# The seam of a two-phase ConvNeXt V2 block: other sums for the last block, another order for the second phase

## The chip, the cores and the metric

The kernel runs on one NeuronCore of a Trainium2 chip. The metric is device time in microseconds (us) of one execution, the median of several. A lower number is better. The profile is of one execution, taken by the hardware profiler.

Engines: PE (TensorE, matrix products), ACT (ScalarE, here GELU), DVE (VectorE), POOL (GpSimd) and SP (SyncE, here a queue that issues DMA transfers). PE writes to PSUM, the accumulator memory of eight banks; the others read from there and from SBUF.

## What is computed

A ConvNeXt V2 block on a 512 x 512 image with 96 channels in bf16: a depthwise 3x3 convolution, a layer norm over channels, an expansion to 384 channels with GELU, a global response norm (GRN) and a projection back, with the input added.

```python
out = zeros_like(x)                       # depthwise 3x3 with zero padding
for i in range(3):
    for j in range(3):
        out = out + xp[:, i:i+H, j:j+W, :] * dw[i, j]
h = _layernorm(out, axis=-1)
h = gelu(einsum('bhwc,ce->bhwe', h, w1))
gx = sqrt((h * h).sum(axis=(1, 2), keepdims=True) + 1e-6)
nx = gx / (gx.mean(axis=-1, keepdims=True) + 1e-6)
h = grn_gamma * (h * nx) + grn_beta + h
return x + einsum('bhwe,ec->bhwc', h, w2)
```

The GRN needs, for each of the 384 expanded channels, the sum of squares over all 262,144 pixels before the projection of the first pixel can be made. That splits the kernel into two phases.

## The kernel before

The image is cut into 128 blocks of 4 rows (2048 pixels). A block has four quarters of 512 pixels. A quarter's expansion is 1536 columns of PSUM, three banks, for 128 partitions.

*First phase.* For each block, in order: convolution on PE, squares, layer norm statistics, the normalised block `yn` written to DRAM and read back as `ynT` (one of six ring buffers, channels on partitions), then the expansion and GELU. The sum of squares of the expanded values is made in one of two ways for each quarter:

- channel-major (`cm_unit`): channels stand on partitions, three matmuls of 512 columns, and DVE takes statistics of each of the three channel chunks (`entry`: one `bn_stats` into the tile `bst`, 32 entries to a group). `aggregate(k)` condenses a group into `mom2` and `tot2`.
- pixel-major (`px_unit`): pixels stand on partitions, six matmuls that cover the same columns, and PE makes products of each 128-column piece with itself ("Gram products", twelve for a quarter) that add up in the tile `gram`. Its diagonal is the sum of squares. These products are kept in a list, `grams`, and `gram_next(n)` emits n of them at a place that suits.

`cm_quads(q)` (line 105) says how many of a block's quarters are channel-major. The expanded values of most blocks are not kept. Three kinds exist:

- "whole" blocks (36): all four quarters channel-major, stored to DRAM (`g_dram`) and reloaded in the second phase (`load_g`);
- "held" blocks (8, among the last 14): they stay in SBUF;
- "made" blocks (84): expanded again in the second phase (`recompute`, line 317) from `yn`, read again from DRAM by `load_yn`, or from ring buffers for the three `KEPT` ones, 122, 126 and 127.

The last blocks, from 114 on, run in `mlp_tail` (line 707), one quarter after the other.

*The seam*, lines 1048 to 1095: the rest of the Gram products, the last group's `aggregate`, `second_moments` (five DVE operations over all groups), four units of recomputation (`advance(4, PRE)`), the sums of the groups, the diagonal of `gram` (three operations, `junk` and `dsum`), an inverse square root by Newton steps on a tile of 128 x 3, the mean over channels through a tiny matmul with `ones_f`, and last the weights of the projection times the scale, `W2s`. Then two units more (`advance(LEAD, PRE)`, LEAD is 6).

*Second phase*, `stage_mm2` (line 340): for each block in `ORDER`, four steps ("subs") of twelve matmuls of 96 columns with `W2s` into one of two output banks, each followed on DVE by the addition of the bias (`o_sb <- PS,B2c`); after each second one DVE also adds the input (`xr`). Between the subs PE runs recomputations for later blocks: after each sub, `pace` (line 392) calls `advance` up to a due number. One such unit is three matmuls into one of two PSUM triples (`banks3`) and one GELU on ACT into a buffer `gr`. `advance` stops at a block that is five or more places ahead (`PRE`), or if three buffers are full: a made block can only be started when the third made block before it has been consumed (`GRB` = 3, `used`):

```python
even = LEAD + (n * NSUB + sub + 1) * total / (NSUB * NBLK)
advance(max(due, even), n + PRE)
```

`ORDER` (lines 180 to 192) mixes the made blocks with the "free" ones, whole and held, two of the first to one of the second. Before the change it begins 122, 116 (held), 126, 127, 117 (held), 1, 2, 0 (whole), 4, 5, 3 (whole), and it ends 119, 125 (held). `load_yn` is issued on SP seven blocks ahead, `load_xr` four and `load_g` up to five blocks ahead on POOL. A whole block's reload needs a buffer that two blocks earlier in a chain has held; the first two use the buffers of the held blocks 116 and 117.

Within the first phase, the seam and the first eight blocks of the second, instructions stay on each engine in the order of the program; later ones may be placed by a scheduler. Lines in the profile are mostly L36, because a helper there issues the instruction; groups are told apart by their tiles.

Of the kernel before, what the change touches and what calls it, by code (L numbers as in the profile page):

```python
# [15 lines left out]
NEWTON_ITERS = 2  # L16
# [41 lines left out]
def kernel(  # L58
# [23 lines left out]
    NBLK = H // GR  # L82
# [13 lines left out]
    def is_held(q):  # L96
        return q in HELD

    def is_whole(q):
        return q < TAIL0 and q % 10 in WHOLE or q == TAIL0  # L100

    def after_whole(q):
        return (q - 1) % 10 in WHOLE

    def cm_quads(q):
        if is_whole(q) or is_held(q):
            return NQ
        if q >= TAIL0:
            return 1 if q >= NBLK - 2 else 0
        return 2 if q >= NBLK - 16 or after_whole(q) or q % 10 in (5, 9) else 3  # L110

    whole = [q for q in range(NBLK) if is_whole(q)]
# [48 lines left out]
    ones_f = consts.tile([128, 128], f32, name="ones_f")  # L161
    B2bc_f = consts.tile([128, C], f32, name="B2bc_f")

    NENT = sum(cm_quads(q) for q in range(NBLK - 2))
    NLAST = cm_quads(NBLK - 2) + cm_quads(NBLK - 1)
    GROUPS = [min(32, NENT - k) for k in range(0, NENT, 32)] + [NLAST]
    NACC = len(GROUPS)
    mom2 = consts.tile([128, NCH, NACC, 2, 3], f32, name="mom2")
    tot2 = consts.tile([128, NACC, NCH], f32, name="tot2")
# [10 lines left out]
    free, rest = HELD[:2], HELD[2:]  # L180
    for i, q in enumerate(whole):
        free.append(q)
        if (i + 1) * len(HELD[2:]) // len(whole) > len(HELD[2:]) - len(rest):
            free.append(rest.pop(0))
    assert not rest
    made_q = KEPT + [q for q in range(NBLK) if not is_whole(q) and not is_held(q) and q not in KEPT]
    ORDER = []
    for i, q in enumerate(made_q):
        ORDER.append(q)
        while len(ORDER) - i - 1 < ((i + 1) * len(free) + len(made_q) // 2) // len(made_q):  # L190
            ORDER.append(free[len(ORDER) - i - 1])
    assert sorted(ORDER) == list(range(NBLK))
    nth_made = {q: n for n, q in enumerate(made_q)}
    SLOTS = [q % NYT for q in KEPT + [NBLK - 5, NBLK - 4, NBLK - 3]]
# [8 lines left out]
    with ExitStack() as p1:  # L203
# [113 lines left out]
        def recompute(q, t):  # L317
            if t == 0:
                grp[q]["g"] = late.gr.tile([128, NQ, NCH, QW], bf16, name="gr")
            cm_unit(grp[q]["g"][:, t], grp[q]["ynt"], t, grp[q]["w1"])  # L320
# [50 lines left out]
        PRE = 5  # L371
        YPRE = 7
        XPRE = 4
        LEAD = 6
# [9 lines left out]
        def advance(target, upto):  # L384
            while made[0] < total and made[0] < target:
                n, t = todo[made[0]]
                if n >= upto or nth_made[ORDER[n]] >= used[0] + GRB:
                    break
                recompute(ORDER[n], t)
                made[0] += 1  # L390
# [152 lines left out]
        def stage_stats(b, halves=(0, 1)):  # L543
            k = batch_of[b]
            b0, n = BATCHES[k]
            for h in halves:
                src = ysq.pop(b) if h else ybf[b]
                for g in range(NG):
                    c0 = (b - b0) * NG + g
                    for i in range(NI):  # L550
                        pe.matmul(S[:, h, c0:c0 + (GR - 1) * n * NG + 1:n * NG],
                                  lhsT=src[:, i, g * 128:(g + 1) * 128], rhs=rowsel[:],
                                  start=False, stop=(i == NI - 1), skip_group_check=True)
# [78 lines left out]
        def stage_turn(k):  # L632
            NT = (BATCHES[k][1] * GR * NG + 31) // 32 * 32
            rt = rtpool.tile([128, NS], bf16, name="rt")
            dve.transpose(out=rt[:, :NT], in_=rns.pop(k)[:, :NT])
            rts[k] = rt
# [45 lines left out]
        bsts = {}  # L682
        ents = {}
        e_ = 0
        for q in range(NBLK):
            if q == NBLK - 2:
                e_ = 32 * (NACC - 1)
            ents[q] = e_
            e_ += cm_quads(q)
        gs = {}  # L690
# [5 lines left out]
        def quarter(b, t):  # L696
            return gs[b][t] if isinstance(gs[b], list) else gs[b][:, t]

        def entry(b, j, m):
            k, e = divmod(ents[b] + m, 32)  # L700
            if k not in bsts:
                bsts[k] = bstpool.tile([128, NCH, 32, 6], f32, name="bst")
            dve.bn_stats(out=bsts[k][:, j, e, :], in_=quarter(b, m)[:, j, :])
# [3 lines left out]
        def mlp_tail(b, get):  # L707
            if b == IN_GH:
                gs[b] = late.gh.tile([128, NQ, NCH, QW], bf16, name="gh")[:]
            elif b > IN_GH:  # L710
                gs[b] = late.gr.tile([128, NQ, NCH, QW], bf16, name="gr")[:]
            elif b in IN_XT:
                gs[b] = g_xt
            elif b == IN_XIN:
                gs[b] = g_xin
            elif not is_held(b):
                while len(sums_only) < 2 * NQ:
                    sums_only.append(ypool.tile([128, NCH, QW], bf16, name="y_bf")[:])
                gs[b] = sums_only[:NQ]
                sums_only.extend(sums_only[:NQ])  # L720
                del sums_only[:NQ]
            else:
                gs[b] = gpool.tile([128, NQ, NCH, QW], bf16, name="g")[:]
            for t in range(NQ):
                cm = t < cm_quads(b)
                (cm_unit if cm else px_unit)(quarter(b, t), ynts[b], t)
                gram_next(12 if len(grams) > 24 else 6)
                if cm:
                    for j in range(NCH):
                        entry(b, j, t)  # L730
                if t == 1:
                    for k in get("turn"):
                        stage_turn(k)
                if t == 2:
                    for b2 in get("stats"):
                        stage_stats(b2)
                if t > cm_quads(b):
                    owe_grams(b, (t - 1) * QC, t * QC)
            for k in get("moments"):
                stage_moments(k)  # L740
            if cm_quads(b) < NQ:
                owe_grams(b, (NQ - 1) * QC, NQ * QC)
            if is_whole(b):
                stores.extend((b, h) for h in range(3))
# [61 lines left out]
        grams = []  # L806

        def gram_next(n):
            for b, c0, j in grams[:n]:
                c = c0 % QC + j * 128  # L810
                v = quarter(b, c0 // QC).rearrange("p j w -> p (j w)")[:, c:c + 128]
                pe.matmul(gram[:, j, :], lhsT=v, rhs=v, start=False, stop=True, skip_group_check=True)
            del grams[:n]

        def owe_grams(b, c0, c1):
            grams.extend((b, c, j) for c in range(c0, c1, E) for j in range(NCH))

        def aggregate(k):
            bst = bsts.pop(k)
            n = 2 * GROUPS[k]  # L820
            v = bst[:].rearrange("p j e (h s) -> p j (e h) s", h=2)[:, :, :n]
            for j in range(NCH):
                dve.bn_stats(out=mom2[:, j, k].rearrange("p h s -> p (h s)"), in_=v[:, j, :, 1])
            dve.tensor_reduce(out=tot2[:, k, :], in_=v[:, :, :, 2], axis=AX.X, op=ALU.add)

        def combine(b):
            for k in sorted(bsts):
                if k < NACC - 1 and (b >= NBLK - 3 or ents[b + 1] >= 32 * (k + 1)):
                    aggregate(k)

        def second_moments(k0, k1):
# [52 lines left out]
        for s in range(last_slot + 1):  # L884
# [73 lines left out]
            else:  # L958
                b = mlp[0]
# [88 lines left out]
        while stores:  # L1048
            store_next()
        gsm = p2.enter_context(tc.tile_pool(name="gsm", side="right", bufs=1))  # L1050
        gram_next(len(grams))
        aggregate(NACC - 1)
        second_moments(0, NACC)
        advance(4, PRE)
        sums = gsm.tile([128, NCH], f32, name="sums")
        dve.tensor_reduce(out=sums[:], in_=parts[:].rearrange("p j k h -> p j (k h)"), axis=AX.X, op=ALU.add)
        for j in range(NCH):
            junk = bstpool.tile([128, 128], f32, name="junk")
            dve.scalar_tensor_tensor(out=junk[:], in0=gram[:, j, :], scalar=1.0, in1=ident_f[:],
                                     op0=ALU.mult, op1=ALU.mult, accum_out=dsum[:, j:j + 1])  # L1060
# [4 lines left out]
        dve.tensor_scalar(out=gi[:], in0=ssq[:].bitcast(i32), scalar1=-0.5, scalar2=float(0x5F3759DF),  # L1065
                                op0=ALU.mult, op1=ALU.add)
        r = gi[:].bitcast(f32)
        for it in range(3):
            t_ = gsm.tile([128, NCH], f32, name=f"gt{it}")
            dve.scalar_tensor_tensor(out=t_[:], in0=r, scalar=-0.5, in1=r, op0=ALU.mult, op1=ALU.mult)  # L1070
            dve.tensor_tensor(out=t_[:], in0=t_[:], in1=ssq[:], op=ALU.mult)
            rn_ = gsm.tile([128, NCH], f32, name=f"gr{it}")
            dve.scalar_tensor_tensor(out=rn_[:], in0=t_[:], scalar=1.5, in1=r, op0=ALU.add, op1=ALU.mult)
            r = rn_[:]
# [17 lines left out]
                                    op0=ALU.mult)  # L1092
        dve.tensor_copy(out=B2c[:], in_=B2bc_f[:])

        advance(LEAD, PRE)
    with p2:
        def out_part(q, o_sb, v):
            r0 = q * GR
# [58 lines left out]
```

## Time and profile before

| | us |
|---|---|
| median of 3 runs | 1434.84 (1434.36 to 1438.47) |
| the profiled execution | 1430.97 |
| its span, first to last instruction | 1429.2 |
| last GELU of the first phase ends | 936.6 |
| first sub of the second phase starts | 944.36 |
| last sub starts, about | 1424.3 |

The first line of the page's part 1 gives the busy time of each engine and its share of the span:

```profile
PE 1378.1 (96%) x23332; PEld 827.4 (58%) x23332; DVE 1304.8 (91%) x2396; ACT 1381.4 (97%) x1693; POOL 887.7 (62%) x735
```

In the second phase the groups by line are, with busy time, mean duration in ns, and idle time before:

```profile
L36 ACT ACTIVATE gr<-PS 128x1536 bf16<-128x1536 f32 x332 | 463.2, 1449 | 12.4 <-PE PS L36 6.3
L36 DVE TENSOR_TENSOR o_sb<-PS,B2c 128x384 bf16<-128x384 f32 x512 | 280.7, 556 | 57.7 <-PE PS L36 52.8
L36 PE MATMUL PS<-ynT,w1s 128*128 128x512 bf16 x972 | 262.7, 379 | 0.0
L36 PE MATMUL PS<-W2s,gr 128*128 128x96 bf16 x4032 | 209.7, 206 | 1.0 <-DVE o_sb L36 0.4
```

[...] Busy shares are averages over both phases, so a place is read from a timeline or a window of that place.

### The profile page before, as it was taken

To read this page: it belongs to the slowest core of one execution; us is meant where nothing else is said; L and a number is where in the kernel's file an instruction comes from. 1 tells how busy PE (TensorE), PEld (TensorE's weight loads), DVE (VectorE), ACT (ScalarE), POOL (GpSimd) and SP (SyncE) were. 2 spreads that over 40 slices of the span, in tenths; PEclk is the share of its full clock that TensorE was granted. 3 is DMA by queue.
4 is the path that set the end of the run, shared out by engine and by line. 5 is a ranking of instruction groups with operands and counts; after the bars stand their busy time and mean duration, and the time that the engine had idled before them with its cause. 6 is when DMAs were issued, how large, how long until landed. Compare 5 with 4: busy or idle time off the path is not lost.

```text
span 1429.2 us, 54985 instructions
## 1 busy us (share of the span) xinstructions
PE 1378.1 (96%) x23332; PEld 827.4 (58%) x23332; DVE 1304.8 (91%) x2396; ACT 1381.4 (97%) x1693; POOL 887.7 (62%) x735
## 2 busy tenths in 40 slices
PE   8899999999999999999999997799999999999998
PEld 3445455545555555554545554367777777777776
DVE  8859999999999999999999998988888888888888
ACT  7899999999999999999999999999999999999996
POOL 3559999999999999999999997302111111111110
PEclk9999999999999999999999999999999999999999
DMA  6577989898998888999889877649999999999996
GB/s 193 174 227 228 274 265 288 263 273 255 283 269 274 260 269 249 267 269 276 271 257 282 262 232 232 198 161 414 419 385 414 401 407 398 413 390 394 395 405 272
DMA packets 167565, 423.64 MB, mean 296 GB/s; under 512 B 34167, under 2 KB 83767, under 8 KB 162711
## 3 DMA queue, kind: packets, MB, share of 16 engines
q1 hardware_dynamic: 151652, 314.59, 69.0%
q0 software_dynamic: 15104, 105.39, 18.5%
q8 instruction: 182, 2.98, 0.9%
q14 instruction: 65, 0.52, 0.1%
q10 hardware_dynamic: 562, 0.15, 0.1%
HBM read 262.16 MB, written 157.79 MB: 294 GB/s over the span
## 4 chain that ended last, share of the span: by engine, by line
PE 58%; ACT 16%; DVE 13%; DMA 6%; POOL 3%; SPq 2%; issue 2%; ACTq 0%; POOLq 0%; DVEq 0%
PE PS L36 58%; ACT g L36 12%; DVE bst L36 8%; ACT y_bf L36 4%; DMA yn_dram<-yn 3%; DVE xT L36 2%; DMA xin<-in_x_dram 2%; SPq L36 2%; POOL ysq L36 1%; DVE o_sb L36 1%; POOL yn L36 1%; DMA ynT<-yn_dram 1%; DVE y_bf L36 1%; ACT ysq L36 0%; DVE mom L36 0%
## 5 line engine op out<-in xcount | busy, mean ns | idle before, releaser
L36 ACT ACTIVATE g<-PS 128x512 bf16<-128x512 f32 (+2 forms) x1160 | 703.6, 780 | 3.7 <-PE PS L36 3.4
L36 DVE BATCH_NORM_STATS2 bst<-g 128x6 f32<-128x512 bf16 x1020 | 623.5, 675 | 23.2 <-ACT g L36 22.5
L36 ACT ACTIVATE gr<-PS 128x1536 bf16<-128x1536 f32 x344 | 479.7, 1456 | 14.0 <-PE PS L36 7.9
L36 POOL TENSOR_TENSOR yn<-y_bf,rbc 128x1536 bf16<-128x1536 bf16 x126 | 391.6, 3110 | 50.6 <-ACT rbc L36 21.4
L36 PE MATMUL PS<-ynT,w1p 128*128 128x512 bf16 x1110 | 341.2, 381 | 16.7 <-ACT g L36 8.7
L36 PE MATMUL PS<-xT,Wq 64*32 64x511 bf16 (+1 forms) x9198 | 336.5, 386 | 12.1 <-ACT g L36 3.0
L36 DVE TENSOR_TENSOR o_sb<-PS,B2c 128x384 bf16<-128x384 f32 x512 | 280.7, 556 | 57.7 <-PE PS L36 52.8
L36 POOL TENSOR_TENSOR ysq<-y_bf 128x1536 bf16<-128x1536 bf16 x114 | 313.5, 2750 | 31.4 <-ACT y_bf L36 22.4
L36 PEld LDWEIGHTS <-g 128*128 128x128 bf16 (+1 forms) x3603 | 217.8, 98 | 119.1 <-issue 37.6
L36 PE MATMUL PS<-ynT,w1s 128*128 128x512 bf16 x972 | 262.7, 379 | 0.0
L295 POOL DMA_DIRECT2D xr<-in_x_dram x116 | 62.2, 536 | 286.3 <-DVE o_sb L36 286.3
L36 PEld LDWEIGHTS <-gr 128*128 128x128 bf16 x4104 | 201.0, 98 | 53.8 <-issue 1.5
L36 PE MATMUL PS<-W2s,gr 128*128 128x96 bf16 x4032 | 209.7, 206 | 1.0 <-DVE o_sb L36 0.4
L36 ACT ACTIVATE y_bf<-PS 128x1536 bf16<-128x1536 f32 (+2 forms) x147 | 184.1, 1274 | 13.0 <-PE PS L36 8.9
L36 DVE STREAM_TRANSPOSE xT<-xin 128x576 f32<-128x576 f32 (+1 forms) x256 | 181.8, 750 | 5.9 <-PE PS L36 4.9
L36 PEld LDWEIGHTS <-w1p 128*128 128x128 bf16 x1110 | 94.9, 97 | 158.7 <-issue 113.8
L36 PEld LDWEIGHTS <-Wq 64*32 64x32 bf16 x9216 | 104.6, 90 | 130.4 <-ACT g L36 61.5
L36 PE MATMUL PS<-g 128*128 128x128 bf16 x1632 | 158.2, 220 | 4.3 <-DVE PS L36 4.1
L36 DVE TENSOR_TENSOR o_sb<-o_sb,xr 128x768 bf16<-128x768 bf16 x256 | 142.8, 558 | 8.9
L36 PE MATMUL PS<-w1p,ynT 128*128 128x384 bf16 (+1 forms) x924 | 141.3, 273 | 7.0 <-ACT y_bf L36 2.0
L36 PEld LDWEIGHTS <-ynT 128*128 128x128 bf16 x924 | 73.0, 97 | 58.4 <-issue 35.5
L36 PE MATMUL PS<-W2s,g 128*128 128x96 bf16 x1968 | 103.7, 206 | 0.2
(114 smaller groups left out, 656.8 us busy)
## 6 DMA issues: line engine op xcount, KB each, us to landing
g<-g_dram POOLq DMA_DIRECT2D x36, 1536.0 KB, 9.8
xin<-in_x_dram SPq DMA_DIRECT2D x126, 432.0 KB
g_dram<-g SPq DMA_DIRECT2D x105, 512.0 KB
yn_dram<-yn SPq DMA_DIRECT2D x512, 96.0 KB
ynT<-yn_dram SPq DMA_DIRECT2D x128, 384.0 KB
out_dram<-o_sb SPq DMA_DIRECT2D x127, 384.0 KB
xr<-in_x_dram POOLq DMA_DIRECT2D x124, 384.0 KB, 7.6
ynT<-yn_dram SPq DMA_DIRECT2D x243, 128.0 KB
```

The lines of the kernel that those rows point to most:

```text
L36: r = f(*a, **k)
L295: pq.dma_start(out=xr[:], in_=x[0, r0:r0 + GR].rearrange("r w c -> (r w) c").rearrange("(p g) c -> p g c", g=PXP))
```

## The change

Four parts, all around the seam:

1. `cm_quads`: block 127 has no channel-major quarter any more; its first quarter goes the pixel-major way too. The last group of statistics, which held one entry each of blocks 126 and 127, is gone; the entry of 126 joins the group before, and that group is aggregated after block 127. `mlp_tail` emits twelve Gram products a quarter for blocks 126 and 127 where it emitted six.
2. The seam is in another order: one unit of recomputation ahead of the second moments and of the last Gram products, then, after these, units up to the third; the fourth stands after `W2s` in the program. Four units are made ahead of the first sub where there were six; `LEAD`, the pace's constant, stays 6.
3. Two Newton steps instead of three.
4. `ORDER`: the two held blocks 116 and 117 come first. The rest is spread anew. It now begins 116, 117, 122, 126, 127, 0 (whole), 1, 2, 3 (whole), 4, 5, 7 (whole), 6, 8, and still ends 119, 125.

```diff
@@ cm_quads
-            return 1 if q >= NBLK - 2 else 0
+            return 1 if q == NBLK - 2 else 0
@@ groups of statistics
-    NENT = sum(cm_quads(q) for q in range(NBLK - 2))
-    NLAST = cm_quads(NBLK - 2) + cm_quads(NBLK - 1)
-    GROUPS = [min(32, NENT - k) for k in range(0, NENT, 32)] + [NLAST]
+    NENT = sum(cm_quads(q) for q in range(NBLK))
+    GROUPS = [min(32, NENT - k) for k in range(0, NENT, 32)]
@@ order of the second phase
+    lead, free = free[:2], free[2:]
...
-        while len(ORDER) - i - 1 < ((i + 1) * len(free) + len(made_q) // 2) // len(made_q):
+        while len(ORDER) - i - 1 < i * len(free) // (len(made_q) - 1):
             ORDER.append(free[len(ORDER) - i - 1])
+    ORDER = lead + ORDER
@@ entries
-            if q == NBLK - 2:
-                e_ = 32 * (NACC - 1)
@@ mlp_tail
-                gram_next(12 if len(grams) > 24 else 6)
+                gram_next(12 if len(grams) > 24 or b >= NBLK - 2 else 6)
@@ combine
-                if k < NACC - 1 and (b >= NBLK - 3 or ents[b + 1] >= 32 * (k + 1)):
+                if b == NBLK - 1 or ents[b + 1] >= 32 * (k + 1):
@@ the seam
-        gram_next(len(grams))
-        aggregate(NACC - 1)
+        assert not bsts
+        advance(1, PRE)
         second_moments(0, NACC)
-        advance(4, PRE)
         sums = gsm.tile([128, NCH], f32, name="sums")
         dve.tensor_reduce(out=sums[:], in_=parts[:].rearrange("p j k h -> p j (k h)"), axis=AX.X, op=ALU.add)
+        gram_next(len(grams))
+        advance(3, PRE)
...
-        for it in range(3):
+        for it in range(NEWTON_ITERS):
...
-        advance(LEAD, PRE)
+        advance(4, PRE)
```

## The prediction

> **What bounds the kernel now.** I read the slices of the page first (TensorE, PE, is at 9 tenths almost throughout, ScalarE, ACT, beside it), then the busy time by windows around the place that the change touches: the end of the first phase and the start of the second. Columns: window, length, busy time with count of PE, weight loads, VectorE (DVE), ACT, GpSimd (POOL), then clock, DMA share, GB/s.
>
> ```profile
> 925.00:937.00 12.00, 9.63 (x107) 7.20 (x106) 12.00 (x27) 11.60 (x9) 0.00 (x0) 1.00 0.61 218
> 937.00:944.00 7.00, 4.80 (x28) 2.16 (x26) 5.69 (x38) 5.82 (x5) 0.00 (x0) 1.00 0.00 0
> 1000.00:1050.00 50.00, 49.91 (x751) 37.54 (x748) 43.28 (x81) 48.50 (x36) 8.58 (x16) 1.00 1.02 415
> 1415.00:1430.00 15.00, 8.37 (x158) 7.08 (x154) 10.63 (x21) 4.08 (x3) 0.00 (x0) 0.91 0.28 107
> ```
>
> From 944 to 1415 PE has no gap (49.91 of 50); ACT is close behind (48.50). So the second phase lasts as long as its PE work, and a time saved or lost at its start reaches the end unchanged. The chain of waits, read next, says the same: it is PE alone from piece to piece, 447 matmuls in 30.08 us.
>
> ```profile
> 933.61 3.56 DVE bst L36 x6
> 937.44 0.24 DVE parts L36
> 939.02 0.64 DVE junk L36 x6
> 946.40 26.76 PE PS L36 x393
> 1035.10 30.08 PE PS L36 x447
> ```
>
> The chain passes over DVE from 911 to 942: the sums of the last blocks (`bst`) run behind ACT, and all scales of the second phase hang on them. The timeline of that stretch (start, duration, engine, what, count, idle before) shows the prices:
>
> ```profile
> 933.52 3.65 DVE L36 BATCH_NORM_STATS2 bst<-gr 128x6 f32<-128x512 bf16 x6
> 936.65 0.84 PE L36 MATMUL PS<-gr 128*128 128x128 bf16 x12 [0.20 <-ACT gr L36]
> 937.08 0.29 DVE L36 BATCH_NORM_STATS2 mom<-bst 128x6 f32<-128x4 f32 x3
> 937.34 1.46 PE L36 MATMUL PS<-ynT,w1p 128*128 128x512 bf16 x6
> 938.18 37.60 ACT L36 ACTIVATE gr<-PS 128x1536 bf16<-128x1536 f32 x27 [1.58 <-PE PS L36]
> 938.94 0.28 DVE L36 SCALAR_TENSOR_TENSOR junk<-PS,ident_f 128x128 f32<-128x128 f32 x1
> 941.26 0.16 DVE L36 SCALAR_TENSOR_TENSOR gt<-gr 128x3 f32<-128x3 f32 x1
> 941.85 0.16 DVE L36 SCALAR_TENSOR_TENSOR gx<-ssq,gr 128x3 f32<-128x3 f32 x1
> 943.15 0.56 DVE L36 TENSOR_SCALAR W2s<-w_sb,sc 128x96 bf16<-128x96 bf16 x3
> 944.36 0.67 PE L36 MATMUL PS<-W2s,gr 128*128 128x96 bf16 x12
> ```
>
> Call three matmuls of 512 columns for one quarter of a block, with their GELU, a unit, and twelve matmuls of 96 columns with W2s a sub. In the gapless stretch a unit follows the next work after 0.643 us of PE and a sub after 0.511. This agrees with the chain: 447 matmuls are 21.4 units and 31.9 subs at the program's ratio of 336 to 512, so 13.8 + 16.3 = 30.1 us. A unit costs ACT 1.345 us (units start at 939.68, 941.03, 942.37, 943.71, each when ACT frees a PSUM triple), with 1.45 from its start to its end. Before the first sub, six units are done.
>
> **The change, part by part.** All times are of the profiled execution: span 1429.2 us, 1430.97 with what lies around it, 3.87 under the median of the runs, 1434.84, to which I add the difference.
>
> *Sums.* Block 127's first quarter is no longer read by DVE: three statistics at 3.65 / 6 = 0.61 us go, and the extra group's three statistics and reduction too. DVE ends block 126's three at 933.22 + 1.83 = 935.05 (the earlier group's aggregation, now larger by one entry, comes behind them). From there to the diagonal sums it needs what it needed from 937.08 to 938.94, 1.86 us: 936.9. PE gets 12 Gram products more (42 columns of time each: 0.69 us from 936.65 to 937.34 for twelve) and six matmuls for three in that quarter at the same columns (0.81 us busy either way, rows at 931.28 and 929.93). In that stretch PE waits 0.19 to 0.53 us per quarter for ACT, whose step is 1.345: a quarter with 12 products, 0.643 + 0.69 = 1.33, still fits, so ACT hides them and I take nothing; without that cover it is 0.7.
>
> *Order at the seam.* PE now runs one unit ahead of the last 24 products. Its PSUM is free when the last but one quarter leaves ACT (936.60 - 1.345 = 935.25), so it runs 935.3 to 935.95, and the products end at 935.95 + 2 x 0.69 = 937.35. Diagonal sums start at 937.5 instead of 938.94: 1.44 earlier, PE now being what they wait for. ACT no longer idles 1.58 us.
>
> *Two Newton steps.* Three operations go, 941.26 to 941.85: 0.59 us. From the diagonal sums to the end of W2s were 943.71 - 938.94 = 4.77 us, now 4.18: ready at 941.7. Units 2 and 3 are done at 938.8 (ACT frees the triple at 936.6 + 1.45), the matmul for the mean of gx at 940.3, unit 4 at 941.05. So the first sub starts at 941.75 instead of 944.36: -2.6 us.
>
> *Fewer units ahead.* Four instead of six: 2 x 0.643 = +1.3 us, made up later on the gapless PE.
>
> *A burst.* The pace is unchanged (line 395: 6.7 units due after the first sub), so three units follow that sub at once. The first runs from 942.25, the second to 943.55, the third needs the triple of the first, whose GELU starts at 942.25 + 0.84 = 943.1 and ends at 944.55: 1.05 us of PE waiting. After the next sub a unit waits for the second GELU (944.45 + 1.45 = 945.9 against 945.7): 0.2. Together +1.25.
>
> *A held pace.* Two held blocks lead, so the first made block's buffer comes free after block 2 instead of block 0, and `GRB` = 3 stops units at 12. Counted through `advance`, subs 1 to 3 of block 2 would bring 1, 1, 0 units and now bring 0, 0, 2. Four subs stand in a row: DVE needs 0.56 for each and 0.56 per pair, while the rows at the end, where only subs are left, show pairs in 1.53 us for PE's 1.02; the two output banks take up part, and I take 0.3 of the 1.0. Then two units, a sub, a unit: it waits for the first GELU (0.84 + 1.45 = 2.29 after that unit's start, against 2 x 0.643 + 0.511 = 1.80): 0.5; the one after it 0.2. Together +1.0. This limit binds nowhere later, by the same count.
>
> *New order.* Blocks stand at other places, with the same work. Reads of yn are issued seven blocks before their block's place. The made blocks now stand up to two places later at the start, while their units' times hardly move: a read's room shrinks from 4.5 to 5.25 blocks to 3.5 to 4.25 for some twenty blocks, and from the middle it is as before. A block lasts (1424.9 - 944.36) / 128 = 3.75 us, so the room is 13.1 us. Packet records of the trace show these reads done 2.5 to 7.9 us after their first packet, which came 2.2 us behind the issue at 949.89. Covered; if not, it is the last rival. Reloads of g land in 8.3 to 11.3 us and have at least four blocks, 15 us, as four of them had before. One third of a read is put early in SP's queue, before the output of block 3; it waits for a unit that runs in block 3's first sub, and that output waits for block 3's end: nothing behind it is late. The order ends with the same two blocks, and units end in the same block: the last ten subs stay.
>
> [...]
>
> **Sum:** -2.6 + 1.3 + 1.25 + 1.0 = +0.95 us, 0.07%: no change that can be told (0.3%, 4.3 us, is what a measurement of this kernel tells from none). 1434.84 + 0.95 = 1435.8. Bounds: if the waits of the burst and the held pace are hidden, -1.3 (1433.5); if the seam gives only Newton's 0.59 and the lost cover costs 0.7, +0.95 + 2.0 + 0.7 = +3.65 (1438.5).
>
> **The rivals.**
> - *The seam's gain is kept* (-1.3, 1433.5): ACT starts 1.58 us earlier and so is ahead when the burst comes. For it: ACT has 1.5 us in 50 to spare. Against: two PSUM triples let it be ahead by two units only.
> - *The change does not shorten the chain* (+3.65, 1438.5): the longer last group or ACT holds the diagonal sums. For it: DVE has 12.00 of 12 busy there. Against: 2.3 us of its work go.
> - *Reads come late* (slower): a yn read that takes over 13.1 us from its issue stops PE at the unit that uses it. Nine made blocks have room of at most 3.75 blocks; 0.5 us each is 4.5, with the seam 1434.84 + 0.95 + 4.5 = 1440.3. For it: DMA share is 1.0 from 960 on, and reloads begin two blocks earlier in the order. Against: 10 us were enough.
> - *Clearly faster* (under 1430.5): the median lies 3.87 above the profiled execution for reasons that the trace does not hold; if some stand at the seam, they may go. In the trace PE idles only 2.2 us of 937 to 944.
>
> **How the numbers follow.** Forecast 0.45, gain kept 0.25, chain not shortened 0.10: all within 0.3%, so same 0.80. Late reads 0.12: slower. Clearly faster 0.08. The three runs span 4.1 us, so a median may lie 2 off. The range reaches 2 to 2.5 us below the kept gain and 1.5 above the unshortened chain, 1431 to 1440; most of the last two rivals is left out.
>
> **What would show it.** In the new profile: first sub near 941.8, 2.6 earlier, behind four units, diagonal sums near 937.5, ACT without its 1.58 us; PE waiting for ACT about 1 us after the first sub, and again some 13 us later after four subs in a row; then no gap up to the end. A PE wait for yn or g after 960, a first sub after 943, or bursts without waits would make the steps wrong.

## The result and the profile after

| | before | after |
|---|---|---|
| median of 7 runs each, us | 1434.71 (1431.73 to 1438.47) | 1441.47 (1435.24 to 1448.29) |
| ratio, 95% interval | | 1.0049 [1.0029, 1.0069] |
| profiled execution's span | 1429.2 | 1438.9 |
| block 126's first GELU starts ("first phase") | 925.45 | 934.02 |
| from there to the first sub | 18.91 | 16.02 |
| from the first sub to the end | 484.84 | 488.86 |

The changed kernel is 0.5% slower; 1441.47 lies above the forecast range of 1431 to 1440. Of the 9.7 us between the two spans 8.6 arise before block 126, where both kernels have the same instructions in the same order on each engine. The rest, 504.88 against 503.75, is +1.1 us.

First the chain of waits of the changed kernel (start, duration, what), at the seam and in the second phase:

```profile
937.16 8.92 PE PS L36 x117
946.10 0.73 DVE junk L36 x6
950.04 2.19 PE PS L36 x15
952.30 1.46 ACT gr L36
984.68 30.08 PE PS L36 x447
```

The seam's chain now goes over PE (the Gram products) to the diagonal sums, no longer over `bst`, and the wait for ACT behind the first sub is in it. The steady stretch costs the same, 30.08 us. Its timeline:

```profile
941.80 1.86 DVE L36 BATCH_NORM_STATS2 bst<-gr 128x6 f32<-128x512 bf16 x3
946.10 0.29 DVE L36 SCALAR_TENSOR_TENSOR junk<-PS,ident_f 128x128 f32<-128x128 f32 x1 [0.62 <-PE PS L36]
949.74 0.56 DVE L36 TENSOR_SCALAR W2s<-w_sb,sc 128x96 bf16<-128x96 bf16 x3
950.04 0.90 PE L36 MATMUL PS<-W2s,g 128*128 128x96 bf16 x12 [0.33 <-DVE W2s L36]
950.77 2.73 PE L36 MATMUL PS<-ynT,w1p 128*128 128x512 bf16 x6
952.30 10.97 ACT L36 ACTIVATE gr<-PS 128x1536 bf16<-128x1536 f32 x8 [1.10 <-PE PS L36]
953.80 0.99 PE L36 MATMUL PS<-ynT,w1p 128*128 128x512 bf16 x3 [0.31 <-ACT gr L36]
961.44 2.50 PE L36 MATMUL PS<-W2s,gr 128*128 128x96 bf16 x48
964.69 10.97 ACT L36 ACTIVATE gr<-PS 128x1536 bf16<-128x1536 f32 x8 [1.41 <-PE PS L36]
```

Counted from 934.02, the diagonal sums start at 12.08 (13.49 before) and the first sub at 16.02 (18.91). Three units follow the first sub, and four subs stand in a row at 961.44, both as counted. New is that the first sub takes 0.90 us instead of 0.67 and six matmuls of the units 2.73 instead of 1.46. For the six matmuls the windows say why (the clock stands third from the end); the sub comes further down.

```profile
946.60:950.00 3.40, 1.82 (x9) 0.69 (x8) 2.54 (x20) 3.04 (x3) 0.00 (x0) 1.00 0.00 0
950.00:953.40 3.40, 3.36 (x18) 1.48 (x18) 0.97 (x4) 2.30 (x2) 0.00 (x0) 0.62 0.00 0
1000.00:1050.00 50.00, 49.92 (x742) 37.36 (x741) 43.23 (x81) 48.47 (x36) 8.99 (x18) 1.00 1.02 417
```

The granted clock fell to 0.62 of full in the 3.4 us behind the first sub, right after a stretch in which PE was busy for 1.82 of 3.4 us.

In the first phase (10 to 925 us), the waits of the two kernels that differ, before and then after (total us, times, longest):

```profile
PE PS L36 <- DVE PS L36: 4.1, 6, 1.4
...
DVE xT L36 <- DMA xin<-in_x_dram: 0.9, 1, 0.9
```

```profile
PE PS L36 <- DVE PS L36: 9.6, 11, 2.4
DVE xT L36 <- DMA xin<-in_x_dram: 7.9, 6, 2.9
```

In this pair of profiles the transposition of x waited for x to be loaded six times instead of once. Nothing in the change touches these loads. What the change does move is memory: with one group of statistics less, `mom2`, `tot2` and `parts` are smaller, and the tiles allocated behind them (`ynT`, then the five `g` buffers of 12,288 bytes per partition, then `bst`) stand 128 bytes lower. `g` moves from byte 47744 to 47616 = 93 x 512.

### The profile page after: what moved, and what is told of

Same layout as the page of the kernel before. It is cut to its first block, busy times and chain, and to the rows that moved or that the text cites. A ratio compares the mean times of both kernels' runs of the same rounds, so it can differ in the third digit from the quotient of the medians.

```text
span 1438.9 us, 55003 instructions
## 1 busy us (share of the span) xinstructions
PE 1383.1 (96%) x23347; PEld 829.1 (58%) x23347; DVE 1302.3 (91%) x2386; ACT 1382.5 (96%) x1693; POOL 887.8 (62%) x735
## 4 chain that ended last, share of the span: by engine, by line
PE 57%; ACT 18%; DVE 15%; DMA 5%; issue 2%; SPq 1%; POOL 1%; ACTq 0%; DVEq 0%; POOLq 0%
PE PS L36 57%; ACT g L36 12%; DVE bst L36 10%; ACT y_bf L36 4%; DVE xT L36 3%; DMA xin<-in_x_dram 3%; DMA yn_dram<-yn 2%; SPq L36 1%; DVE y_bf L36 1%; DVE o_sb L36 1%; DMA rbc<-r_dram 1%; POOL yn L36 0%; ACT ysq L36 0%; ACT gh L36 0%; ACT gr L36 0%
## 5 line engine op out<-in xcount | busy, mean ns | idle before, releaser
L36 ACT ACTIVATE g<-PS 128x512 bf16<-128x512 f32 (+2 forms) x1160 | 704.4, 779 | 9.4 <-PE PS L36 8.8
L36 DVE BATCH_NORM_STATS2 bst<-g 128x6 f32<-128x512 bf16 x1020 | 622.8, 674 | 23.0 <-ACT g L36 22.5
L36 ACT ACTIVATE gr<-PS 128x1536 bf16<-128x1536 f32 x344 | 479.7, 1456 | 15.2 <-PE PS L36 9.2
L36 POOL TENSOR_TENSOR yn<-y_bf,rbc 128x1536 bf16<-128x1536 bf16 x126 | 391.2, 3107 | 61.0 <-ACT rbc L36 21.7
L36 PE MATMUL PS<-ynT,w1p 128*128 128x512 bf16 x1107 | 342.6, 384 | 14.9 <-ACT g L36 6.9
L36 PE MATMUL PS<-xT,Wq 64*32 64x511 bf16 (+1 forms) x9198 | 337.2, 387 | 12.1 <-ACT g L36 3.1
L36 DVE TENSOR_TENSOR o_sb<-PS,B2c 128x384 bf16<-128x384 f32 x512 | 280.3, 556 | 61.4 <-PE PS L36 56.2
L36 POOL TENSOR_TENSOR ysq<-y_bf 128x1536 bf16<-128x1536 bf16 x114 | 313.2, 2747 | 29.1 <-ACT y_bf L36 22.6
L36 PEld LDWEIGHTS <-g 128*128 128x128 bf16 (+1 forms) x3603 | 217.8, 98 | 124.9 <-issue 44.3
L36 PE MATMUL PS<-ynT,w1s 128*128 128x512 bf16 x972 | 262.5, 379 | 0.5 <-ACT gr L36 0.4
L36 PEld LDWEIGHTS <-gr 128*128 128x128 bf16 x4116 | 202.1, 98 | 54.3 <-issue 1.1
L36 PE MATMUL PS<-W2s,gr 128*128 128x96 bf16 x4032 | 210.6, 206 | 1.1 <-DVE o_sb L36 0.4
L36 ACT ACTIVATE y_bf<-PS 128x1536 bf16<-128x1536 f32 (+2 forms) x147 | 183.9, 1273 | 14.6 <-PE PS L36 10.5
L36 DVE STREAM_TRANSPOSE xT<-xin 128x576 f32<-128x576 f32 (+1 forms) x256 | 181.8, 750 | 14.8 <-DMA xin<-in_x_dram 7.9
L36 PEld LDWEIGHTS <-w1p 128*128 128x128 bf16 x1107 | 95.0, 98 | 157.3 <-issue 112.2
L36 PEld LDWEIGHTS <-Wq 64*32 64x32 bf16 x9216 | 104.4, 90 | 131.1 <-ACT g L36 59.5
L36 PE MATMUL PS<-g 128*128 128x128 bf16 x1632 | 158.3, 220 | 9.8 <-DVE PS L36 9.6
L36 DVE TENSOR_TENSOR o_sb<-o_sb,xr 128x768 bf16<-128x768 bf16 x256 | 142.7, 557 | 8.9
L36 PE MATMUL PS<-w1p,ynT 128*128 128x384 bf16 (+1 forms) x930 | 142.6, 273 | 6.4 <-ACT y_bf L36 2.0
L36 PEld LDWEIGHTS <-ynT 128*128 128x128 bf16 x930 | 73.7, 98 | 58.5 <-issue 36.0
L36 PE MATMUL PS<-W2s,g 128*128 128x96 bf16 x1968 | 103.8, 206 | 0.5 <-DVE W2s L36 0.3
```

The costliest lines, as they stand in the source:

```text
L36: r = f(*a, **k)
```

## Experiments

Ratios are to the kernel before, run in the same set; one profile each. `warm` and `order_back` have that one execution alone, so no ratio. "First phase" is as in the table above. "33rd" is the time from the first bias addition of the second phase to the 33rd: 30.85 us in the kernel before.

**Is it the program or scatter? Is it the addresses?** `null_before` and `null_after` are the two kernels again.

> The kernel before, unchanged. What its own scatter is. All theories: ratio to before 1.000 within its interval; first phase (to the start of block 126's GELU) 925 us, as in the profile of before. If the first phase alone scatters by several us between profiled executions of one program, the first phase here is off 925.45 by 2 us or more.

> The changed kernel, unchanged. If its 6.8 us are a property of the program: ratio again 1.003 to 1.007, first phase again near 934 us in the profile. If they are scatter of the first phase that fell on this kernel's runs: ratio 1.000 to 1.002 (the seam's own 1 us), first phase anywhere from 925 to 936.

```diff
 after_pad: changed kernel
     dsum = consts.tile([128, NCH], f32, name="dsum")
+    pad = consts.tile([128, 32], f32, name="pad")
```

> The changed kernel with 128 bytes of unused room per partition behind its small tiles, so that ynT and g stand at the addresses that they have in the kernel before (one group of statistics less had moved them down by 128 bytes). Theory of addresses: the first phase is back at 925 us and the ratio at 1.001. Theory of scatter: the same as the changed kernel's repeat within the intervals. Theory that the seam alone costs it: the same as the repeat.

```diff
 before_shift: kernel before
-    gam = consts.tile([128, NCH], f32, name="gam")
-    dsum = consts.tile([128, NCH], f32, name="dsum")
     gpool = ctx.enter_context(tc.tile_pool(name="g", bufs=5))
+    fin = ctx.enter_context(tc.tile_pool(name="fin", bufs=1))
+    dsum = fin.tile([128, NCH], f32, name="dsum")
+    gam = fin.tile([128, NCH], f32, name="gam")
...
-        warm = consts.tile([32, 32], bf16, name="warm")
+        warm = fin.tile([32, 32], bf16, name="warm")
```

> The kernel before with three small tiles moved behind g, so that ynT and g stand 128 bytes lower, at the changed kernel's addresses. Theory of addresses: first phase near 934 us, ratio 1.004 to 1.006. Theory of scatter, and of the seam: ratio 1.000.

**Which tile, and is it the multiple of 512?** `g_back` and `g_half` put an unused tile of 128 and 64 bytes between `ynT` and `g`; `g_lower` makes `before_shift`'s move in the changed kernel; `after_third` is the changed kernel once more.

```diff
 g_back: changed kernel (g_half: 16 instead of 32)
+    gap = ctx.enter_context(tc.tile_pool(name="gap", bufs=1)).tile([128, 32], f32, name="gap")
     gpool = ctx.enter_context(tc.tile_pool(name="g", bufs=5))
```

> The changed kernel with 128 unused bytes between ynT and g: g is back at its address of the kernel before, ynT stays 128 bytes lower. If g's address makes the first phase longer: first phase 925 to 927 us in the profile, ratio as with both back, 1.0008. If ynT's does: first phase 929 to 934, ratio as the changed kernel's repeat, 1.002 or more. If addresses do nothing and the first batch was scatter, the ratio is anywhere from 1.000 to 1.003, with no tie to the address.

> The changed kernel with three small tiles moved behind g: g (and ynT) another 128 bytes lower, g at 47488, 384 above a multiple of 512. If a multiple of 512 is what is slow: ratio 1.000 to 1.001, first phase 925 to 927 us. If a lower place is what is slow, or this is scatter that the address does not set: 1.002 or more, or no pattern.

> The changed kernel with 64 unused bytes ahead of g: g at 47680, 64 above a multiple of 512. If only the multiple of 512 is slow: ratio 1.000 to 1.001, first phase 925 to 927 us. If slowness fades step by step from 0 to 128 bytes: ratio about 1.0015.

> The changed kernel unchanged, a third set of runs. If g's place at a multiple of 512 bytes makes the first phase longer: ratio 1.002 to 1.005 again, first phase 928 us or more. If the earlier two sets were scatter: ratio 1.000 to 1.001.

| kernel | seam and order | g, bytes above a multiple of 512 | ratio, 95% interval | first phase, us |
|---|---|---|---|---|
| changed | new | 0 | 1.0049 [1.0029, 1.0069] | 934.0 |
| null_after | new | 0 | 1.0022 [1.0006, 1.0038] | 929.7 |
| after_third | new | 0 | 1.0025 [1.0012, 1.0038] | 927.8 |
| before_shift | old | 0 | 1.0024 [1.0008, 1.0041] | 931.4 |
| null_before | old | 128 | 1.0007 [0.9993, 1.0022] | 928.2 |
| after_pad | new | 128 | 1.0008 [0.9993, 1.0023] | 925.1 |
| g_back (ynT low) | new | 128 | 0.9997 [0.9986, 1.0008] | 925.9 |
| g_half (ynT low) | new | 64 | 1.0004 [0.9992, 1.0017] | 927.7 |
| g_lower (ynT lower still) | new | 384 | 0.9990 [0.9974, 1.0006] | 929.0 |

In this table all four sets with `g` at a multiple of 512 lie above 1 with their whole interval; of the five others every interval holds 1. Single pairs overlap, so the weight lies in the pattern: the 35 executions of `null_after`, `after_third` and `before_shift` lie on average 0.23% above the median of the kernel before in their set, the 59 of the five others 0.03%, a difference of 0.20% (2.9 us) with a standard error of 0.04%. The old program with only its addresses changed (`before_shift`) is as slow as the changed one's two repeats; the changed program at other addresses is not slower than the kernel before. So the greater part of the repeated loss follows the place of `g`, not the seam; `ynT`'s place does not matter (`g_back`), and lower is not slower (`g_lower`). `bst` moves too, but it stands at its old place in `before_shift`, which is slow, and at the changed kernel's in `g_lower`, which is not. The sizes expected were larger: 1.003 to 1.007 for `null_after` and 1.004 to 1.006 for `before_shift`. The first phase of a single execution scatters, in the kernel before too (925.45 and 928.2), so that column supports the ratios but carries no verdict: `g_lower` and `g_half` missed the 925 to 927 expected of them. The profiles of the versions below fit in: 924.8 to 927.3 for the six with `g` off a multiple, 929.2 for `st_off`, which has it on one. The first set of the changed kernel, 1.0049, was larger than its repeats, 1.0022 and 1.0025; no run explains that surplus.

The instructions that use `g` take the same time in both places (100 to 900 us: GELU into `g` 685 and 687 ns, statistics from `g` 674 and 675 ns). The transfers differ, though not cleanly: in the packet records of that stretch the 3456-byte packets, of which only the loads of x consist, take 172 to 182 ns on average in the four multiple-of-512 profiles of the table, 164 to 169 in the five others except the first profile of before (177); the slowest twentieth of the 4096-byte ones begins at 368 to 384 ns against 347 to 365. Of the versions below, `st_off`, on a multiple, has 167 ns and `st_mult`, off it, 173. Nor is late x what the slow profiles share: the wait for it is 7.9 us in the changed kernel and 3.9 in `before_shift`, but 1.7 and 0.9 in the two repeats. PE's wait for DVE in the first phase (`PE PS L36 <- DVE PS L36`) separates the four, 5.3 to 9.6 us, from the five others, 3.1 to 4.6; `st_off` has 4.3.

**Which access to g?** The stores of `g` to DRAM are the transfers that touch it in this phase. Their cuts were moved:

```diff
 st_off: changed kernel; st_mult, st_ctl: after_pad, with 192 and 64
-                sp.dma_start(out=g_dram[whole.index(b)][:, h * n:h * n + n],
-                             in_=flat(b)[:, h * n:h * n + n])
+                c0, c1 = [0, n + 64, 2 * n + 64, 3 * n][h:h + 2]
+                sp.dma_start(out=g_dram[whole.index(b)][:, c0:c1], in_=flat(b)[:, c0:c1])
```

> The changed kernel (g at a multiple of 512 bytes), each whole block's three stores cut at 0, 4224 and 8320 bytes instead of 0, 4096 and 8192: two of three start 128 bytes above a multiple of 512. If the stores' start decides: ratio 1.000 to 1.001. If the engines' accesses to g decide: 1.002 to 1.005 as the changed kernel.

> The changed kernel at the old addresses (g 128 bytes above a multiple of 512), stores cut at 0, 4480 and 8576 bytes: two of three start at a multiple of 512. If the stores' start decides: ratio 1.0015 to 1.003, two thirds of the changed kernel's surplus. If the engines' accesses decide: 1.000 to 1.001.

> The changed kernel at the old addresses, stores cut at 0, 4224 and 8320 bytes: none starts at a multiple of 512. Control for the uneven cut: 1.000 to 1.001 by both theories; more would mean that the cut itself costs time (in DRAM too the starts are moved).

Measured: `st_off` 1.0007 [0.9994, 1.0021], `st_mult` 1.0010 [0.9998, 1.0022], `st_ctl` 1.0016 [1.0005, 1.0028]. The control, without a start on a multiple, is the slowest of the three and lies above 1 with its whole interval, so the cut seems to have a price of its own, and the three do not separate the theories. They also break the pattern of the table: `st_off` has `g` at a multiple of 512, cuts its stores as unevenly as the control, and is not slower than it, though the intervals overlap. So what is shown of the place of `g` is shown for the kernels with evenly cut stores, and that the stores' start decides is neither shown nor excluded.

**The parts of the seam.** `warm` fills PE's idle stretch, `order_back` restores the order, both from `after_pad`:

```diff
 warm
         advance(3, PRE)
+        for _ in range(7):
+            pe.matmul(PS[:, 6, 128:512], lhsT=w1p[:, :128], rhs=w1p[:], start=True, stop=True)
 order_back
-    lead, free = free[:2], free[2:]
...
-        while len(ORDER) - i - 1 < i * len(free) // (len(made_q) - 1):
+        while len(ORDER) - i - 1 < ((i + 1) * len(free) + len(made_q) // 2) // len(made_q):
...
-    ORDER = lead + ORDER
```

> The changed kernel at the old addresses with seven matmuls of 384 columns (about 1.1 us, results unused) behind the third unit, where PE idles 1.3 us. If idling there drops the clock: granted clock 1.00 in the 30 us around the seam (0.94 in the three profiles of changed kernels), first sub 0.67 us busy instead of 0.9 to 1.3, the three units behind it with 0.64 us steps, and 488.4 us or less from the first sub to the end instead of 488.9 to 489.2. If the clock drops for another reason: 0.94 again.

> The changed kernel at the old addresses with the second phase's order of the kernel before; all else as changed. Theory of the held pace: the wait near block 2 (four subs in a row, then a unit that waits for ACT) is gone, 1.0 us, so 488.0 us from the first sub to the end. Rival (order costs nothing): 489 again. The burst behind the first sub and the half clock stay.

The timeline of `warm`, with the seven matmuls at 938.56:

```profile
938.56 1.30 PE L36 MATMUL PS<-w1p 128*128 128x384 bf16 x7
...
942.13 1.46 PE L36 MATMUL PS<-ynT,w1p 128*128 128x512 bf16 x6
943.03 10.97 ACT L36 ACTIVATE gr<-PS 128x1536 bf16<-128x1536 f32 x8 [0.47 <-PE PS L36]
944.53 0.81 PE L36 MATMUL PS<-ynT,w1p 128*128 128x512 bf16 x3 [0.94 <-ACT gr L36]
```

The six matmuls are back at 1.46 us, and what is left is the pure wait for the PSUM triple, 0.94 us. The clock of the 30 us around the seam is 1.00 in all three profiles with the filling, 0.94 in six of eleven of the new seam without it. So an unfilled seam can lose the clock, and does not always.

The clock records show which executions lose it. Up to the kernel's last microseconds each stretch at half clock lasts 3.413 us or a multiple (in the changed kernel 6.827 us from 237.414, 3.413 from 868.880 and from 950.800; in the kernel before 3.413 from 860.724), and within one execution they start on a raster of that step: the three of the changed kernel lie 185 and 24 steps apart. Two raster windows at the seam of the changed kernel, then one each of `st_ctl` and `null_before`, which kept the clock (clock third from the end):

```profile
947.39:950.80 3.41, 1.81 (x18) 1.18 (x19) 2.27 (x16) 3.20 (x3) 0.00 (x0) 1.00 0.00 0
950.80:954.21 3.41, 3.10 (x12) 0.97 (x9) 0.56 (x1) 2.31 (x3) 0.00 (x0) 0.50 0.00 0
```

```profile
938.73:942.14 3.41, 2.12 (x20) 1.14 (x18) 2.28 (x17) 3.17 (x3) 0.00 (x0) 1.00 0.02 5
```

```profile
941.38:944.80 3.41, 1.78 (x7) 0.48 (x5) 2.93 (x21) 3.41 (x3) 0.00 (x0) 1.00 0.00 0
```

In the six profiles that lost the clock the window just ahead of the fall has PE busy for 1.79 to 1.98 us; there the window holds most or all of the 1.3 us gap and the 0.33 us gap ahead of the first sub. In the five that kept it these two gaps fall into different windows, and the emptiest one has 2.12 or 2.13. So within the new seam the place of the raster goes with the loss, but busy time alone is not the rule: `null_before`, with the old seam, kept the clock with 1.78. And the filling is not shown to have saved it. In `warm` and `best_again` the raster stands where unfilled profiles kept the clock too (a window begins 4.3 and 4.6 us ahead of the first sub, against 4.1 to 4.6 in those that kept it and 2.5 to 3.4 in those that lost it); `best`, at 3.6, lies between.

The first sub's 0.67 did not come back (0.89, and 0.89 to 0.90 in the unfilled profiles that kept the clock): it starts when the first third of `W2s` is ready and ends after the last (in the changed kernel `W2s` is written from 949.74 to 950.30, 0.24 us a third, and the sub runs from 950.04 to 950.94). In `order_back` the four subs in a row are gone; only two stand together at that place:

```profile
952.73 1.18 PE L36 MATMUL PS<-W2s,gr 128*128 128x96 bf16 x24
953.75 0.81 PE L36 MATMUL PS<-ynT,w1s 128*128 128x512 bf16 x3
```

Up to the 33rd addition: changed kernel 34.77, `warm` 34.14, `order_back` 33.05 (whose clock stayed at 1.00 by itself). The four unfilled profiles with the new order that kept the clock (`g_half`, `st_off`, `st_mult`, `st_ctl`) also show 34.14. So the half clock cost 0.63 us and the held pace 34.14 - 33.05 = 1.09. The remaining 33.05 - 30.85 = 2.20 is the two units and the burst together; with the units at 2 x 0.643 = 1.29, 0.91 is left for the burst, beside the 0.94 us wait in the timeline of `warm`. To the end `order_back` took 489.84 from its first sub, nearer to its rival's 489 than to the 488.0 expected. The difference came later: after the 33rd addition it needed 451.72 us against 448.88 before, with DVE waiting 4.2 us for output transfers and PE 3.0 for DVE. Late transfers come in other kernels too. In `null_before`, the kernel before, the waits of 1040 to 1270 us hold

```profile
DVE o_sb L36 <- DMA out_dram<-o_sb: 2.2, 3, 1.2
PE PS L36 <- DMA ynT<-yn_dram: 1.4, 2, 0.8
```

and it needed 487.99 us from the first sub instead of 484.84. The rival of late reads thus exists, but as scatter of both kernels, not as an effect of the new order: in six of the seven profiles of the changed seam and order that got neither the filling nor other store cuts (changed, `null_after`, `after_third`, `after_pad`, `g_half`, `g_lower`; the seventh, `g_back`, lost 0.7) the time from the 33rd to the last bias addition was 448.83 to 448.93, in the profile of before 448.88.

**A version from the parts:** old addresses, old order, filling, five units ahead (`advance(5, PRE)` for the last `advance(4, PRE)`), two sets.

> From the changed kernel: old addresses (128 bytes of room), the old order of the second phase, five units ahead of the first sub instead of four, seven matmuls of 384 columns into a free bank while PE waits at the seam (results unused). Theory (seam as in the sum, clock lost by the idle stretch, held pace by the order): first sub 16.2 us after block 126's first GELU starts (18.91 before, 16.0 changed), no half clock there, from the first sub to the end 486.0 us (484.84 before, 488.9 changed); the sum 1.5 us better than before, ratio 0.999. Rival (the waits come from fewer units alone): 487.5 or more after the first sub, ratio 1.000.

> The version with old addresses, old order, five units ahead and filled idle time, a second set of runs. If its gain is real: ratio 0.998 to 0.9995 with the interval below or at 1, and from block 126's first GELU to the 33rd bias addition 49.4 us as before (50.5 in the kernel before). If the first set was luck: 1.000.

Its 33rd addition came at 32.48 and the first sub at 16.22 in both sets; from block 126's first GELU to the 33rd addition it needed 49.43 us, as expected, 1.04 less than the kernel before. The ratios were 0.9980 [0.9959, 1.0001] and 0.9995 [0.9982, 1.0008], from the first sub to the end 486.32 and 487.22 us (486.0 expected). The first ratio is more than the 1 us at the seam gives, the second about as much; both intervals hold 1, so it cannot be told from the kernel before.

## Why the prediction was wrong

- *The step that failed* is the last one of the sum, "to which I add the difference": +0.95 us was added to the median as if the first phase stayed as it was, a term put at nothing without a reason. Its instructions did stay. But part 1 of the change shrinks three tiles, `g` lands on a multiple of 512 bytes, and the first phase gets longer: over the sets of repeats that place of `g` costs 2.9 us. Repeats put the whole change at 1.0022 and 1.0025 (3.2 and 3.6 us), of which about 1.1 belong to the seam. No term and no rival stood for this; "clearly faster" was the only one that went beyond the trace of one execution, and it pointed the other way.
- *What stays open.* In the first set the loss was 6.8 us, some 3 more than in the repeats, and no run shows why. The medians of the repeats, 1438.22 and 1436.39, lie inside the range, so without that surplus the place of `g` alone would not have carried the time out of it. By which access the place of `g` acts is open too.
- *Sums and order at the seam* held: diagonal sums 1.41 us earlier (1.44 forecast), DVE then waiting 0.62 us for PE.
- *Newton*: from the diagonal sums to the end of `W2s` 4.20 us, forecast 4.18.
- *First sub*: it starts 2.89 us earlier, forecast 2.6, because it needs only the first third of `W2s` where the forecast let it wait for the last. It then takes longer, and the first bias addition is 2.67 us earlier.
- *Two units fewer and the burst*: together 2.20, forecast 1.3 + 1.25 = 2.55. *Held pace*: 1.09, forecast 1.0.
- *Not forecast at the seam*: the half clock, 0.63 us. From block 126's first GELU to the end the three profiles of the unchanged "after" show 504.74 to 504.88, +1.0 to +1.1 against the first profile of before. That this meets the forecast's +0.95 is in part luck: all three have the half clock. The four that kept it (`g_half`, `st_off`, `st_mult`, `st_ctl`) show 504.1 to 504.3, +0.4 to +0.5. The terms were right in kind, the burst was taken too large, and the half clock filled the difference.
- *New order* held as "same work"; reads and reloads were not later than before. "The seam's gain is kept" fell (both waits are there), "the change does not shorten the chain" too.
- Two slips in the prediction change nothing: at 336 units to 512 subs, 447 matmuls are 21.0 units and 32.0 subs, 29.9 us and not 30.1 beside the chain's 30.08; and a Gram product's 0.69 / 12 = 57 ns is about 137 columns at the unit's pace (0.643 us for 1536), not 42.
- At other places of `g` the changed kernel is 0.9990 to 1.0008 with evenly cut stores: no change that can be told, which is what the forecast said of the seam alone.

## To carry to other kernels

A change in the size of one small tile can move every tile allocated behind it, here by 128 bytes; when a stretch that the diff does not touch gets slower, compare addresses, and put padding back as an experiment. Compare the executions phase by phase at a mark that both share: here that separated 8.6 us from 1.1 at once. And run the old kernel against itself: its own scatter (1.0007 [0.9993, 1.0022]) is what any ratio has to beat. A set of seven executions, as here the first, can lie some 3 us off its repeats.

## What the hardware showed that was not expected

- The place of a buffer in SBUF alone was worth some 0.2%: four sets with `g` at a multiple of 512 bytes at 1.0022 to 1.0049, five others at 0.9990 to 1.0008, all with evenly cut stores. With unevenly cut stores the difference did not show (1.0007 on a multiple, 1.0010 and 1.0016 off it). What makes the first phase longer there stays open.
- PE's clock fell with PE half busy: 1.81 of 3.41 us in the raster window before the fall, and no gap over 1.3 us. The kernel before kept it with 1.78 of 3.41 in `null_before`. Ahead of the last microseconds every stretch at half clock lasted 3.413 us or a multiple (6.827 once in the changed kernel). The stretches lie on a raster that stands elsewhere in each execution: in the eleven profiles of the new seam without the filling a window begins 2.5 to 4.6 us ahead of the first sub. Where it put the two gaps of the new seam, 1.3 and 0.33 us, into different windows the clock was kept, in five of five; where one window held most or all of both it was lost, in six of six. By what rule the clock falls is not shown.
